# Later weight copies and squares, a reserve of channel matmuls, six raw buffers: a fused attention and mixer kernel on one Trainium2 core

## The chip, the core and the metric

The kernel runs on one core of a Trainium2 chip. A core has a matrix engine (TensorE, "PE" in the profile, with weight loads in a row of their own, "PEld"), a vector engine (VectorE, "DVE"), a scalar engine (ScalarE, "ACT"), GpSimd ("POOL") and SyncE ("SP"). Each works through its own list of instructions in order; between engines there are semaphores. PE reads SBUF and writes PSUM. PSUM is handed out in banks. Data comes from and goes to DRAM by DMA, which an engine issues and 16 DMA engines carry out.

The metric is the device time of one execution in microseconds (us). Lower is better.

## The reference

Eight batches, 12 heads, 448 tokens, head size 64. Attention without a softmax (squared ReLU of the scores) is followed by an MLP mixer: a token mix over the 448 tokens (hidden 256) and a channel mix over the 768 channels (hidden 1536).

```python
def _attn_ref(q, k, v):
    S = q.shape[2]
    scale = 1.0 / np.sqrt(q.shape[-1])
    scores = scale * np.matmul(q, k.transpose(0, 1, 3, 2))
    attn = np.maximum(scores, 0.0) ** 2 / S
    return np.matmul(attn, v)

def _moe_ref(x, w_tok1, w_tok2, w_ch1, w_ch2):
    xt = x.transpose(0, 2, 1)
    h = np.maximum(xt @ w_tok1, 0.0) @ w_tok2
    u = x + h.transpose(0, 2, 1)
    h2 = np.maximum(u @ w_ch1, 0.0) @ w_ch2
    return u + h2
```

All inputs and the output are float32 in DRAM; the kernel computes in bfloat16 with float32 sums, and the loads convert.

## The kernel before

**Pairs and iterations.** The unit of attention work is a pair of heads: six pairs a batch (`NP`), 48 pairs in all. The main loop (L399) runs over s = 0 to 51. In iteration s the work of several pairs is interleaved, so that each step's inputs were made some iterations earlier:

- scores of pair s: three blocks of 128 keys, each with both heads (`sc_ps`, L186), and the remaining 64 keys of both heads together (`sr_ps`, L200). For each block `relu2` (L172) puts a ReLU on ACT (`at`, L175) and a square on DVE (`sq`, L176);
- transposes of q and k of pair s+1 on PE (`qkT_ps`, L159) and the copy to `qkT` on DVE (L169), which the scores of iteration s+1 read;
- values of pair s-1 (`acc_ps`, L216 and L224) and the scaling into `xT` on DVE (L232);
- x_back of pair s-2: PE transposes `xT` (`x_ps`, L250), DVE copies it to `x_sb` (L258);
- for odd s token1, for even s token2, of two pairs at once (`PG` = 2): `t_ps` (L268) with a ReLU on ACT (L276), then `h_ps` (L286) and an add on DVE that makes `uT_sb` (L294).

**Order.** The order on each engine is the order in which the program emits instructions; nothing is rearranged (`manual_schedule`). An iteration emits: scores of blocks 0 and 1 with their ReLUs and squares; the loads of pair s+3; the weight loads due in this iteration; fill; x_back; token2; fill; scores of block 2; transposes; values; rest scores; fill; token1; fill.

**Channel work and fills.** When the last pair of a batch has had its token2 (s = 8, 14, 20, ... 50), `channel_work` puts the batch's channel matmuls into a list, as units: 12 units of channel1 (six matmuls L311 and a ReLU on ACT, L318) and six or eight units of channel2 (12 matmuls L329, three L339, an output copy on DVE, L347; six for an even batch, eight for an odd one). `fill(0.25)` is called four times an iteration. Each call adds 1186 ns to a credit (a quarter of the mean work of a batch over six iterations) and runs units while the credit is above zero, each at its assumed cost: 1134 ns for channel1, 2124 ns for channel2. With an empty list the credit is held at or below zero. After the loop the rest of the list is run.

**PSUM.** `ps_mm` has three banks, which `qkT_ps`, `x_ps`, `t_ps`, `h_ps` and the channel matmuls use in rotation; `ps_att` has two buffers of two banks for the scores, `ps_acc` one.

**Loads.** All loads stand in POOL's queue, in the order of emission. A pair's load is a q, a k and a v load (112, 96 and 96 KB in SBUF); the first pair of a batch adds four loads of the last 64 keys and values of all heads (`load_rest`, 48 KB each, into `kz` and `vz`). Pairs 0, 1 and 2 are loaded before the loop, pair s+3 in iteration s. The pool `raw` has four buffers of each kind, so the v load of pair n waits until the values matmuls of pair n-4 are done. The weights: wt1 at s=0 (seven loads), wt2 at s=1 (one load into `wt2_nat`, then two DVE copies, L125, that reorder it), wc1 in quarters at s=2 to 5, wc2 in quarters at s=6 to 9. The identity for the transposes is made by POOL, after the loads of pair 0 (L392). Outputs are stored from SP's queue.

Of the kernel before, what the change touches and what calls it, by code (L numbers as in the profile page):

```python
# [9 lines left out]
FP32 = mybir.dt.float32  # L10
BF16 = mybir.dt.bfloat16
AF = mybir.ActivationFunctionType
ALU = mybir.AluOpType
# [3 lines left out]
def kernel(  # L17
# [11 lines left out]
    nc = tc.nc  # L29
# [4 lines left out]
    DC = moe_w_ch1.shape[1]  # L34
# [15 lines left out]

    consts = ctx.enter_context(tc.tile_pool(name="consts", bufs=1))
    wpool = ctx.enter_context(tc.tile_pool(name="wpool", bufs=1))
    raw = ctx.enter_context(tc.tile_pool(name="raw", bufs=4))
    attn = ctx.enter_context(tc.tile_pool(name="attn", bufs=2))
    mix = ctx.enter_context(tc.tile_pool(name="mix", bufs=2))
    outp = ctx.enter_context(tc.tile_pool(name="outp", bufs=3))
# [2 lines left out]
    ps_mm = ctx.enter_context(tc.tile_pool(name="ps_mm", bufs=3, space=bass.MemoryType.PSUM))  # L59
# [3 lines left out]
    ident = consts.tile([128, 128], BF16, name="ident")  # L63
# [12 lines left out]
    def load_pair(s):  # L76
        b, p = divmod(s, NP)
        h0 = 2 * p
        q_raw = raw.tile([QP, 2, QC, D], BF16, name="q_raw")
        k_raw = raw.tile([128, 2, KB, D], BF16, name="k_raw")  # L80
        v_raw = raw.tile([128, 2, KB, D], BF16, name="v_raw")
        nc.gpsimd.dma_start(  # L82
            out=q_raw.rearrange("p h c d -> p h (c d)"),
            in_=q[b, h0 : h0 + 2].rearrange("h (p c) d -> p h (c d)", c=QC),
        )
        nc.gpsimd.dma_start(  # L86
            out=k_raw.rearrange("p h c d -> p h (c d)"),
            in_=k[b, h0 : h0 + 2, :KM].rearrange("h (p c) d -> p h (c d)", c=KB),
        )
        if p == 0:  # L90
            load_rest(b, kz[b % 2], k)
        nc.gpsimd.dma_start(  # L92
            out=v_raw.rearrange("p h c d -> p h (c d)"),
            in_=v[b, h0 : h0 + 2, :KM].rearrange("h (p c) d -> p h (c d)", c=KB),
        )
        if p == 0:
            load_rest(b, vz[b % 2], v)
        raws[s] = (q_raw, k_raw, v_raw)

    def load_rest(b, dst, src):  # L100
        for e in range(2):
            nc.gpsimd.dma_start(
                out=dst[64 * e : 64 * e + KR, :, D * e : D * (e + 1)],
                in_=src[b].rearrange("(p e) s d -> e s p d", e=2)[e, KM:],
            )

    def load_wt1():
        w = moe_w_tok1.rearrange("(p c) j -> c p j", c=QC)
        for c in range(QC):
            lo = c * QP  # L110
            while lo < (c + 1) * QP:
                hi = min((c + 1) * QP, (lo // 128 + 1) * 128)
                r = lo % 128
                nc.gpsimd.dma_start(
                    out=wt1[r : r + hi - lo, lo // 128, :],
                    in_=w[c, lo - c * QP : hi - c * QP, :],
                )
                lo = hi

    def load_wt2():  # L120
        nc.gpsimd.dma_start(
            out=wt2_nat, in_=moe_w_tok2.rearrange("(c j) s -> j c s", c=JC)
        )
        for j in range(JC):
            nc.vector.tensor_copy(  # L125
                wt2[:, j, :].rearrange("n (c p) -> n c p", c=QC),
                wt2_nat[:, j, :].rearrange("n (p c) -> n c p", c=QC),
            )

    def load_wc1(i):  # L130
        n = DC // 4
        nc.gpsimd.dma_start(
            out=wc1[:, :, i * n : (i + 1) * n],
            in_=moe_w_ch1.rearrange("(g p) n -> p g n", p=128)[:, :, i * n : (i + 1) * n],
        )

    def load_wc2(i):
        n = EC // 4
        nc.gpsimd.dma_start(
            out=wc2[:, i * n : (i + 1) * n, :],  # L140
            in_=moe_w_ch2.rearrange("(e p) n -> p e n", p=128)[:, i * n : (i + 1) * n, :],
        )


    qkT, at2, acc = {}, {}, {}
    KO = S

    def transposes(s):
# [23 lines left out]
    def relu2(s, key, ps, n):  # L172
        at = attn.tile([128, n, S], BF16, tag=f"at{n}", name="at", bufs=3)
        sq = attn.tile([128, n, S], BF16, tag=f"sq{n}", name="sq", bufs=3 * (3 if n == 2 else 1))
        nc.scalar.activation(at, ps[:, :, :S], AF.Relu)  # L175
        nc.vector.tensor_tensor(out=sq, in0=at, in1=at, op=ALU.mult)  # L176
        at2[s, key] = sq

    def scores(s, blocks):
        sb = qkT[s]  # L180
        made = []
        for c in blocks:
            ps = ps_att.tile([128, 2, 512], FP32, tag="att", name="sc_ps")
            for e in range(2):
                h = slice(64 * e, 64 * (e + 1))
                nc.tensor.matmul(  # L186
                    ps[:, e, :S],
                    lhsT=sb[h, KO + c * 128 : KO + (c + 1) * 128],
                    rhs=sb[h, :S],
                    start=True,  # L190
                    stop=True,
                )
            made.append((c, ps))
        for c, ps in made:
            relu2(s, c, ps, 2)

    def scores_rest(s):
        sb = qkT.pop(s)
        ps = ps_att.tile([128, 1, 512], FP32, tag="att", name="sr_ps")
        nc.tensor.matmul(  # L200
            ps[:, 0, :S],
            lhsT=sb[:, KO + KM : KO + KM + 128],
            rhs=sb[:, :S],
            start=True,
            stop=True,
        )
        relu2(s, KB, ps, 1)
# [36 lines left out]
    def x_back(s):  # L244
        b, p = divmod(s, NP)
        if p % PG == 0:
            x_tiles[s // PG] = mix.tile([128, 4, PG, 128], BF16, name="x_sb")
        ps = ps_mm.tile([128, 1024], BF16, tag="bank", name="x_ps")
        for c in range(4):
            nc.tensor.matmul(  # L250
                ps[:, c * 128 : (c + 1) * 128],
                lhsT=xT[b % 2][:, p, c * 128 : (c + 1) * 128],
                rhs=ident,
                is_transpose=True,
                start=(c == 0),
                stop=(c == 3),
            )
        nc.vector.tensor_copy(  # L258
            x_tiles[s // PG][:, :, p % PG, :],
            ps[:, :512].rearrange("n (c d) -> n c d", c=4),  # L260
        )
# [100 lines left out]
    queue = []  # L362

    def channel_work(b):
        for e in range(EC):
            queue.append((6 * 189, lambda e=e: channel1(b, e)))
        half = NT // 2
        for t in range(half) if b % 2 == 0 else range(half, NT):
            for i in range(2):
                queue.append((12 * 163 + 3 * 56, lambda t=t, i=i: channel2(b // 2, t, i)))  # L370

    NS = B * NP
    given = [0.0]
    credit = [0.0]
    per_batch = EC * 6 * 189 + NT * (12 * 163 + 3 * 56)

    def fill(share):
        credit[0] += share * per_batch / NP
        while queue and credit[0] > 0:
            cost, unit = queue.pop(0)  # L380
            credit[0] -= cost
            unit()
        if not queue:
            credit[0] = min(credit[0], 0.0)


    PRE = 3
    for i in range(2):
        nc.vector.memset(kz[i], 0.0)
        nc.vector.memset(vz[i], 0.0)  # L390
    load_pair(0)
    make_identity(nc, ident)  # L392
    for i in range(2):
        nc.vector.memset(xT[i][:, :, S:], 0.0)
    nc.vector.memset(wt1[:, 3, :], 0.0)
    load_pair(1)
    load_pair(2)
    transposes(0)
    for s in range(NS + 4):  # L399
        if s < NS:  # L400
            scores(s, (0, 1))
        if s + PRE < NS:
            load_pair(s + PRE)
        if s == 0:
            load_wt1()
        if s == 1:
            load_wt2()
        if 2 <= s < 6:
            load_wc1(s - 2)
        if 6 <= s < 10:  # L410
            load_wc2(s - 6)
        fill(0.25)
        if 0 <= s - 2 < NS:
            x_back(s - 2)
        if 0 <= s - 3 < NS and (s - 3) % PG == PG - 1:
            for i in range(PG):
                token2(s - 3 - (PG - 1) + i)
            if (s - 3) % NP == NP - 1:
                channel_work((s - 3) // NP)
        fill(0.25)  # L420
        if s < NS:
            scores(s, (2,))
        if s + 1 < NS:
            transposes(s + 1)
        if 0 <= s - 1 < NS:
            values(s - 1)
        if s < NS:
            scores_rest(s)
        fill(0.25)
        if 0 <= s - 2 < NS and (s - 2) % PG == PG - 1:  # L430
            token1((s - 2) // PG)
        fill(0.25)
# [32 lines left out]
```

## Time and profile before

| | before |
|---|---|
| median of 3 runs | 452.16 us (451.62 to 452.26) |
| profiled execution | 451.94 us |
| its span, first to last instruction | 450.2 us |
| PE busy | 408.8 us, 91% of the span |
| DVE busy | 231.0 us, 51% |
| ACT busy | 212.3 us, 47% |
| POOL busy | 132.6 us, 29% |
| loads, in POOL's queue | 21.70 MB as written to SBUF |
| stores, in SP's queue | 11.01 MB |

All times below come from the profiled execution, counted from its first instruction; 451.94 - 450.2 = 1.74 us lie outside the span. Matmuls overlap in the array, and the profile models their ends, so a run of matmuls is measured from start to start. Records on DVE overlap by some hundredths too. A timeline row reads: start, duration, engine, line, operation, tile written<-tiles read, sizes, count; in brackets, how long the engine stood idle before it and what ended the wait.

### The profile page before, as it was taken

How to read it: one execution, taken by the hardware profiler on the slowest of the kernel's cores; microseconds unless marked ns; L12 is line 12 of the kernel's file. 1: busy time of each engine (PE TensorE's matmuls, PEld its weight loads, DVE VectorE, ACT ScalarE, POOL GpSimd, SP SyncE). 2: the span in 40 equal slices, each digit the busy share in tenths (PEclk: the TensorE clock that was granted, in tenths of full speed). 3: DMA queues.
4: the chain of work that ended last, by engine and by line, in shares of the span. 5: the costliest groups of instructions: out<-in, count | busy, mean ns of one | idle time of the engine just before them, and what ended most of it. 6: DMA issues, size and time to landing. Idle time of an engine off the chain costs nothing.

```text
span 450.2 us, 8061 instructions
## 1 busy us (share of the span) xinstructions
PE 408.8 (91%) x3336; PEld 218.2 (48%) x3336; DVE 231.0 (51%) x449; ACT 212.3 (47%) x313; POOL 132.6 (29%) x198
## 2 busy tenths in 40 slices
PE   2467799998999989998999989999899989999995
PEld 1134344554455544554445545455445545455563
DVE  3278754565455655556446663555545565443011
ACT  3346756535653456534654337634564436630400
POOL 8837553312511333311431224113333110000000
PEclk9999999999999999999999999999999999999999
DMA  8939999543633635445455446336534532012013
GB/s 80 117 34 168 201 177 123 67 87 64 62 40 65 123 62 52 47 66 105 38 51 78 77 83 66 41 64 90 73 38 56 99 64 45 0 37 58 14 46 96
DMA packets 60517, 33.23 MB, mean 74 GB/s; under 512 B 40832, under 2 KB 56896, under 8 KB 60480
## 3 DMA queue, kind: packets, MB, share of 16 engines
q0 software_dynamic: 56000, 21.70, 43.2%
q1 hardware_dynamic: 4480, 11.01, 8.5%
q8 instruction: 26, 0.43, 0.4%
q14 instruction: 11, 0.09, 0.1%
HBM read 43.38 MB, written 11.01 MB: 121 GB/s over the span
## 4 chain that ended last, share of the span: by engine, by line
PE 77%; ACT 8%; issue 5%; DVE 4%; POOL 4%; DMA 1%; ACTq 0%; DVEq 0%; POOLq 0%
PE m_ps L311 23%; PE m_ps L329 22%; ACT at L175 7%; PE sc_ps L186 6%; PE acc_ps L216 6%; PE qkT_ps L159 5%; PE t_ps L268 4%; PE acc_ps L224 3%; PE m_ps L339 2%; PE h_ps L286 2%; PE sr_ps L200 2%; PE x_ps L250 1%; DVE sq L176 1%; DMA wt_nat<-in_moe_w_tok_dram 1%; DVE out_sb L347 1%
## 5 line engine op out<-in xcount | busy, mean ns | idle before, releaser
L176 DVE TENSOR_TENSOR sq<-at 128x896 bf16<-128x896 bf16 x192 | 108.4, 564 | 136.4 <-ACT at L175 136.4
L175 ACT ACTIVATE at<-sc_ps 128x896 bf16<-128x896 f32 x144 | 125.8, 917 | 84.1 <-PE sc_ps L186 84.1
L329 PE MATMUL m_ps<-wc,r_sb 128*128 128x384 bf16 x672 | 126.5, 326 | 4.6 <-DVE x_sb L258 4.6
L311 PE MATMUL m_ps<-uT_sb,wc 128*128 128x448 bf16 x576 | 120.6, 353 | 6.4 <-DVE x_sb L258 6.3
L92 POOL DMA_DIRECT2D v_raw<-in_v_dram x48 | 34.1, 711 | 233.8 <-PE acc_ps L224 215.3
L311 PEld LDWEIGHTS <-wc 128*128 128x128 bf16 x576 | 54.4, 98 | 61.8 <-issue 16.6
L318 ACT ACTIVATE r_sb<-m_ps 128x448 bf16<-128x448 f32 x96 | 52.5, 547 | 65.3 <-PE m_ps L311 65.3
L329 PEld LDWEIGHTS <-r_sb 128*128 128x128 bf16 x672 | 63.3, 98 | 39.0 <-issue 3.7
L347 DVE COPY out_sb<-m_ps 128x384 f32<-128x384 f32 x56 | 31.2, 556 | 64.5 <-PE m_ps L329 64.5
L186 PE MATMUL sc_ps<-qkT 64*128 64x448 bf16 x288 | 45.8, 369 | 13.0 <-DVE qkT L169 10.1
L175 ACT ACTIVATE at<-sr_ps 128x448 bf16<-128x448 f32 x48 | 26.1, 543 | 33.1 <-PE sr_ps L200 32.9
L216 PE MATMUL acc_ps<-sq,v_raw 128*64 128x448 bf16 x288 | 36.6, 362 | 0.0
L86 POOL DMA_DIRECT2D k_raw<-in_k_dram x48 | 34.9, 728 | 0.0
L169 DVE COPY qkT<-qkT_ps 128x960 bf16<-128x960 bf16 x48 | 31.3, 651 | 4.8 <-PE qkT_ps L159 4.8
L82 POOL DMA_DIRECT2D q_raw<-in_q_dram x48 | 32.7, 682 | 1.1 <-POOLq L449 0.8
L186 PEld LDWEIGHTS <-qkT 64*128 64x128 bf16 x288 | 11.1, 95 | 45.3 <-issue 28.8
L276 ACT ACTIVATE r_sb<-t_ps 128x512 bf16<-128x512 f32 x24 | 14.3, 597 | 33.6 <-PE t_ps L268 33.6
L232 DVE TENSOR_SCALAR xT<-acc_ps 128x448 bf16<-128x448 f32 x48 | 29.6, 616 | 0.7 <-PE acc_ps L224 0.7
L159 PE MATMUL qkT_ps<-ident,q_raw 112*64 112x112 bf16 x384 | 19.4, 225 | 9.3 <-POOL ident masks.py:199 6.8
L294 DVE TENSOR_TENSOR uT_sb<-h_ps,xT 128x448 bf16<-128x448 f32 x48 | 27.5, 615 | 0.0
L286 PE MATMUL h_ps<-wt,r_sb 128*128 128x448 bf16 x96 | 24.3, 352 | 3.3 <-ACT r_sb L318 2.5
L268 PE MATMUL t_ps<-x_sb,wt 128*128 128x256 bf16 x192 | 24.9, 273 | 0.0
(35 smaller groups left out, 265.7 us busy)
## 6 DMA issues: line engine op xcount, KB each, us to landing
q_raw<-in_q_dram POOLq DMA_DIRECT2D x48, 112.0 KB, 3.2
k_raw<-in_k_dram POOLq DMA_DIRECT2D x48, 96.0 KB, 3.3
v_raw<-in_v_dram POOLq DMA_DIRECT2D x48, 96.0 KB, 2.9
wc<-in_moe_w_ch_dram POOLq DMA_DIRECT2D x8, 576.0 KB, 7.2
out_dram<-out_sb SPq DMA_DIRECT2D x8, 336.0 KB, 2.8
out_dram<-out_sb SPq DMA_DIRECT2D x8, 288.0 KB, 2.9
out_dram<-out_sb SPq DMA_DIRECT2D x8, 240.0 KB, 2.8
out_dram<-out_sb SPq DMA_DIRECT2D x8, 192.0 KB, 2.9
```

What stands on the lines that cost most here:

```text
L86: nc.gpsimd.dma_start(out=k_raw.rearrange("p h c d -> p h (c d)"), in_=k[b, h0 : h0 + 2, :KM].rearrange("h (p c) d -> p h (c d)", c=KB),)
L92: nc.gpsimd.dma_start(out=v_raw.rearrange("p h c d -> p h (c d)"), in_=v[b, h0 : h0 + 2, :KM].rearrange("h (p c) d -> p h (c d)", c=KB),)
L159: nc.tensor.matmul(ps[64 * h : 64 * (h + 1), at : at + n], lhsT=src[:, h, :], rhs=ident[:n, :n], is_transpose=True, start=True, stop=True, ...
L175: nc.scalar.activation(at, ps[:, :, :S], AF.Relu)
L176: nc.vector.tensor_tensor(out=sq, in0=at, in1=at, op=ALU.mult)
L186: nc.tensor.matmul(ps[:, e, :S], lhsT=sb[h, KO + c * 128 : KO + (c + 1) * 128], rhs=sb[h, :S], start=True, stop=True,)
L216: nc.tensor.matmul(ps[64 * e : 64 * (e + 1), :S], lhsT=v_raw[:, e, c, :], rhs=sq[:, e, :], start=(c == 0), stop=False, skip_group_check=True,)
L268: nc.tensor.matmul(ps[:, j, :], lhsT=wt1[:, c, j * 128 : (j + 1) * 128], rhs=x_sb[:, c].rearrange("n g d -> n (g d)"), start=(c == 0), sto ...
L311: nc.tensor.matmul(ps[:, :S], lhsT=wc1[:, g, e * 128 : (e + 1) * 128], rhs=uT[:, g, off : off + S], start=(g == 0), stop=(g == CC - 1),)
L318: nc.scalar.activation(r2[:, e, off : off + S], ps[:, :S], AF.Relu)
L329: nc.tensor.matmul(ps[:, :HN], lhsT=r2[:, e, tok], rhs=wc2[:, e, cols], start=(e == 0), stop=(e == EC - 1), skip_group_check=True,)
L347: nc.vector.tensor_copy(o[:, cols], ps[:, :HN])
```

## The change

1. `raw` gets six buffers instead of four.
2. `make_identity` is called inside `load_pair(0)`, after the q and k loads of pair 0 and before the rest loads.
3. The reordering copies of wt2 leave `load_wt2` and become `order_wt2`, called at s=3. The load itself stays at s=1.
4. wc1 is loaded in two halves at s=3 and s=5; the quarters of wc2 go to s=7 to 10.
5. `relu2` no longer emits the square; it notes it, and `square()` emits those noted. It is called after x_back (squares of blocks 0 and 1) and after the rest scores (block 2 and the rest), so behind the qkT copy and the xT scaling.
6. The credit of `fill` starts at -2500 instead of 0, isn't changed while the list is empty, and is no longer held at zero.
7. Ahead of everything DVE clears a tile `warm`, and PE runs nine matmuls 128x512 on it, whose result isn't used.

```diff
-    raw = ctx.enter_context(tc.tile_pool(name="raw", bufs=4))
+    raw = ctx.enter_context(tc.tile_pool(name="raw", bufs=6))
...
+        if s == 0:
+            make_identity(nc, ident)
         if p == 0:
             load_rest(b, kz[b % 2], k)
...
+
+    def order_wt2():
         for j in range(JC):
             nc.vector.tensor_copy(
...
     def load_wc1(i):
-        n = DC // 4
+        n = DC // 2
...
         nc.scalar.activation(at, ps[:, :, :S], AF.Relu)
-        nc.vector.tensor_tensor(out=sq, in0=at, in1=at, op=ALU.mult)
+        squares.append((at, sq))
         at2[s, key] = sq
+
+    def square():
+        for at, sq in squares:
+            nc.vector.tensor_tensor(out=sq, in0=at, in1=at, op=ALU.mult)
+        squares.clear()
...
-    credit = [0.0]
+    RESERVE = 2500.0
+    credit = [-RESERVE]
...
     def fill(share):
+        if not queue:
+            return
         credit[0] += share * per_batch / NP
         while queue and credit[0] > 0:
             cost, unit = queue.pop(0)
             credit[0] -= cost
             unit()
-        if not queue:
-            credit[0] = min(credit[0], 0.0)
...
+    warm = consts.tile([128, 512], BF16, name="warm")
+    nc.vector.memset(warm, 0.0)
     for i in range(2):
         nc.vector.memset(kz[i], 0.0)
         nc.vector.memset(vz[i], 0.0)
+    warm_ps = ps_mm.tile([128, 512], FP32, tag="bank", name="warm_ps")
+    for i in range(9):
+        nc.tensor.matmul(warm_ps, lhsT=warm[:, :128], rhs=warm, start=True, stop=True)
     load_pair(0)
-    make_identity(nc, ident)
...
-        if 2 <= s < 6:
-            load_wc1(s - 2)
-        if 6 <= s < 10:
-            load_wc2(s - 6)
+        if s == 3:
+            order_wt2()
+        if s in (3, 5):
+            load_wc1((s - 3) // 2)
+        if 7 <= s < 11:
+            load_wc2(s - 7)
         fill(0.25)
         if 0 <= s - 2 < NS:
             x_back(s - 2)
+        square()
...
         if s < NS:
             scores_rest(s)
+        square()
         fill(0.25)
```

More of the change, by code (lines that the diff above doesn't have):

```diff
@@ L142, in load_wc2 @@
         )
-    qkT, at2, acc = {}, {}, {}
+    qkT, at2, squares = {}, {}, []
     KO = S
@@ L372 @@
     NS = B * NP
-    given = [0.0]
-    credit = [0.0]
+    RESERVE = 2500.0
+    credit = [-RESERVE]
     per_batch = EC * 6 * 189 + NT * (12 * 163 + 3 * 56)
     def fill(share):
+        if not queue:
+            return
         credit[0] += share * per_batch / NP
```

## The prediction

> **What bounds the kernel now.** I read the chain of work that ended last, then the waits, then the timeline of the places that the waits name.
>
> ```profile
> PE 77%; ACT 8%; issue 5%; DVE 4%; POOL 4%; DMA 1%; ACTq 0%; DVEq 0%; POOLq 0%
> ```
>
> TensorE (PE) holds 77% of the chain. So a gap of PE is worth its length, and work taken off another engine is worth only the PE gaps that it causes. The waits say which gaps there are:
>
> ```profile
> POOL v_raw L92 <- PE acc_ps L224: 215.3, 39, 8.9
> PE sc_ps L186 <- DVE qkT L169: 10.1, 5, 7.5
> DVE wt L125 <- DMA wt_nat<-in_moe_w_tok_dram: 7.7, 1, 7.7
> PE qkT_ps L159 <- POOL ident masks.py:199: 6.8, 1, 6.8
> PE m_ps L311 <- DVE x_sb L258: 6.3, 4, 1.7
> PE m_ps L329 <- DVE x_sb L258: 4.6, 3, 1.5
> ```
>
> Columns: total us, times, longest. PE waits once 7.5 us for a qkT copy, DVE once 7.7 us for a load, and PE seven times, 10.9 us in all, for VectorE's (DVE's) x_sb copy. The long POOL row is a queue held by four raw buffers; no PE wait for a q or k load stands among these, so by itself it costs nothing. First place, the timeline around 19 to 25 us (start, duration, engine, line):
>
> ```profile
> 8.55 0.93 PE L186 MATMUL sc_ps<-qkT 64*128 64x448 bf16 x4 [0.75 <-DVE qkT L169]
> ...
> 18.94 0.73 POOL L121 DMA_DIRECT2D wt_nat<-in_moe_w_tok_dram  x1
> 23.67 0.70 DVE L125 COPY wt<-wt_nat 128x448 bf16<-128x448 bf16 x2 [7.72 <-DMA wt_nat<-in_moe_w_tok_dram]
> 24.82 0.65 DVE L169 COPY qkT<-qkT_ps 128x960 bf16<-128x960 bf16 x1
> 25.53 0.93 PE L186 MATMUL sc_ps<-qkT 64*128 64x448 bf16 x4 [7.51 <-DVE qkT L169]
> 30.35 0.36 PE L186 MATMUL sc_ps<-qkT 64*128 64x448 bf16 x2
> ```
>
> In iteration s=1 the copies of wt2 stand in DVE's queue and wait for wt_nat; the qkT copy of s=2 is behind them, and PE waits for that. Second place, iteration s=6, before channel work exists:
>
> ```profile
> 34.77 0.55 PE L186 MATMUL sc_ps<-qkT 64*128 64x448 bf16 x4
> ...
> 44.48 0.55 PE L186 MATMUL sc_ps<-qkT 64*128 64x448 bf16 x4
> 46.69 0.62 DVE L176 TENSOR_TENSOR sq<-at 128x896 bf16<-128x896 bf16 x1 [0.18 <-ACT at L175]
> 47.23 0.42 DVE L258 COPY x_sb<-x_ps 128x512 bf16<-128x512 bf16 x1
> 47.57 1.15 DVE L294 TENSOR_TENSOR uT_sb<-h_ps,xT 128x448 bf16<-128x448 f32 x2
> 48.63 0.62 DVE L176 TENSOR_TENSOR sq<-at 128x896 bf16<-128x896 bf16 x1
> 49.16 0.65 DVE L169 COPY qkT<-qkT_ps 128x960 bf16<-128x960 bf16 x1
> 49.73 0.62 DVE L232 TENSOR_SCALAR xT<-acc_ps 128x448 bf16<-128x448 f32 x1
> 50.26 0.39 DVE L176 TENSOR_TENSOR sq<-at 128x448 bf16<-128x448 bf16 x1
> ```
>
> From scores to scores runs a DVE chain: two squares (the second at 46.69), x copy, two adds, third square, qkT copy. Third place, the start of a batch's channel work (s=14):
>
> ```profile
> 104.44 0.55 PE L186 MATMUL sc_ps<-qkT 64*128 64x448 bf16 x4
> 105.20 0.93 PE L286 MATMUL h_ps<-wt,r_sb 128*128 128x448 bf16 x4
> 106.79 0.62 DVE L176 TENSOR_TENSOR sq<-at 128x896 bf16<-128x896 bf16 x1 [0.18 <-ACT at L175]
> 107.33 0.41 DVE L258 COPY x_sb<-x_ps 128x512 bf16<-128x512 bf16 x1
> 107.80 1.41 PE L311 MATMUL m_ps<-uT_sb,wc 128*128 128x448 bf16 x6 [1.68 <-DVE x_sb L258]
> ```
>
> No unit was left for the first fill, so the token matmuls follow the scores at once; the x copy sits behind two squares, these behind ACT, and the next unit lacks its bank.
>
> **The change, part by part.** Sums are made on the profiled execution, 451.94 us with a span of 450.2; the median of the runs is 452.16.
>
> *Before s=3: nothing.* Identity goes up the POOL queue: transposes no longer wait 6.8 us for it, but the rest loads of k, v0 and the rest loads of v follow it, later by its two POOL instructions; the first transposes then end on the k rest instead. I take no gain. A loss is covered: after the change DVE needs wt_nat only at s=3, and POOL's order up to that load stays, so it lands at about 23.67 again. Even at the slow pace 25.53 to 30.35 (4.82 us an iteration) s=3 would start by 8.55 + 3 x 4.82 = 23.0. The warm-up memset and nine matmuls stand on engines that wait for the first loads. All this, and the removed wait for raw buffers, buys nothing up to here.
>
> *wt2 copies at s=3.* The wait is not removed, it is moved: DVE stops at s=3, and behind it stand the x copy, two squares and the qkT copy for s=4. From 23.67: copies 0.70, x copy 0.34, squares 2 x 0.54, qkT copy 0.65, 0.1 to PE gives 26.54 for the scores of s=4 (spacings of the rows of s=6). Before they were at 34.77: **-8.2**.
>
> *Squares later, s=4 to 7.* The third square (48.63 to 49.16: 0.53) leaves the chain to qkT, and the x copy (0.34) no longer follows the first two: 0.87 an iteration, 1.74 from 9.71 a pair (34.77 to 44.48), 7.97. DVE's own work in a pair is eight squares (six of 0.54, two of 0.39), two each of qkT (0.57), xT (0.53), x (0.34), adds of 1.06: 3.24 + 0.78 + 2.88 + 1.06 = 7.96, so the next bound is there at once; I take 8.1. Two pairs: 16.2; next are the rows of s=8:
>
> ```profile
> 54.15 0.55 PE L186 MATMUL sc_ps<-qkT 64*128 64x448 bf16 x4
> 57.38 2.55 PE L311 MATMUL m_ps<-uT_sb,wc 128*128 128x448 bf16 x12 [1.54 <-DVE x_sb L258]
> 61.65 2.43 PE L311 MATMUL m_ps<-uT_sb,wc 128*128 128x448 bf16 x12
> 64.02 0.55 PE L186 MATMUL sc_ps<-qkT 64*128 64x448 bf16 x4
> ```
>
> Before, 34.77 to 54.15 is 19.4: **-3.2**. S=8 starts at 42.7. If DVE's queue has a wait that I miss, half of this goes.
>
> *Reserve at s=8.* The credit starts at -2500 and a fill grants 1186, so of s=8's fills only the fourth (the third that grants work after the batch is queued) runs a unit. Before, s=8 took 9.87 with four units of 2.37/2 = 1.19. After: second square ends 2.8 after the scores (46.69 + 0.54 - 44.48), adds end 3.9, one unit 1.2: 5.1. The three units left are done later, 3.6. 5.1 + 3.6 - 9.87 = **-1.2**.
>
> *Loads that run ahead.* POOL now passes pairs 5 and 6 early, and wc1 goes out in two halves.
>
> ```profile
> 40.00:50.00 10.00, 7.54 (x82) 3.95 (x83) 8.42 (x18) 6.92 (x10) 6.82 (x10) 1.00 1.30 183
> 60.00:70.00 10.00, 10.00 (x90) 4.96 (x89) 5.02 (x10) 6.89 (x11) 5.33 (x8) 1.00 1.19 160
> wc<-in_moe_w_ch_dram POOLq DMA_DIRECT2D x8, 576.0 KB, 7.2
> ```
>
> The queue is worked off in order. Behind wt_nat (23.67), up to k of pair 9, by the shapes: five pairs' worth of q, k, v less one v (1.46 MB), four rest loads (0.20) and all of wc1 (2.36): 4.0 MB. At 183 GB/s (last column, weight loads in flight) that is 22 us: 45.6; at 160 it is 48.7. The transposes for s=9 stand in front of values, rest scores and the first unit (1.75 us of PE) and would want pair 9 by 42.7 + 3.9 - 1.75 = 44.9. I take **+0.7**; the ends are 0 and +3.8. The Trainium skill, "DMA: Bandwidth & Descriptors", section "Anatomy of one DMA", gives 2.0 us plus bytes over 436 GB/s, which would land 576 KB in 3.4 us; the row has 7.2, and by that figure of the Trainium skill pair 9 would be early and the sum 432.0.
>
> *Batch boundaries.* Seven waits for x_sb make 10.9; less the 1.54 of s=8, 9.4 in six, 1.56 each. From s=20 on the first fill has a channel2 unit in hand: credit stands at about -1563 when a batch has been worked off, and the 24 fills of a batch end in the boundary's first fill with one more unit to run. That gives ACT and DVE its 2.1 us (12 x 163 + 3 x 56 ns, the source's own cost), and the x copy is no longer behind squares. Next late is the second token matmul, whose bank is that unit's, freed by its out copy:
>
> ```profile
> 91.48 1.20 PE L286 MATMUL h_ps<-wt,r_sb 128*128 128x448 bf16 x4
> ```
>
> 1.20 against the 0.93 at 105.20: 0.27. So 5 x (1.56 - 0.27) = **-6.5**. At s=14 there is no reserve: batch 0 has 6 + 12 units, 26352 ns of work against 28476 - 2500 granted, so its last unit runs one fill early and the queue is empty. There PE passes on to the third scores, transposes and values (some 1.8 us) and then waits for the adds; half of the wait stays: **-0.8**.
>
> *Elsewhere*, the squares now wait behind the x copy, which waits for PE's fill; behind them stand the adds that free two of three banks. One unit of fill (1.19) and the third scores stand before the bank is wanted, two squares take 1.08: I take nothing. The wait for credit itself costs nothing, since PE has no gaps in the tail after s=50 and the reserved units only move there.
>
> Sum: -8.2 - 3.2 - 1.2 + 0.7 - 6.5 - 0.8 = -19.2; 451.94 - 19.2 = **432.7**.
>
> **The rivals.**
> *Cold array.* Scores at 25.53 take 0.93, at 34.77 0.55, though the granted clock is full:
>
> ```profile
> PEclk9999999999999999999999999999999999999999
> ```
>
> Token1 at the full pace is this row:
>
> ```profile
> 53.05 1.03 PE L268 MATMUL t_ps<-x_sb,wt 128*128 128x256 bf16 x8
> ```
>
> So PE runs at about half pace up to 30.35, some 4.8 us after it starts to be busy. If it is still so in s=3, PE ends s=3 at 23.0 + 4.8 = 27.8, token1 at twice 1.03 ends at 29.9, and s=4 starts 3.3 later: 436.0. For it: between the nine matmuls and the scores at 8.55 PE has only transposes. Against: PE is busier from 8.55 to 23 than before. The Trainium skill, "TensorE: Matmul & The Clock Gate", Part 1, says that full rate comes after about 3.4 us of sustained work and is lost after an idle window as long; by that rule the nine matmuls could be undone before the scores begin, which is this rival; the trace agrees with the length of the run-up (4.8 us at 25.53) and with the loss after 7.51 us of waiting, and shows nothing in between.
>
> *Late loads.* At 160 GB/s pair 9 comes at 48.7: +3.1, 435.8.
>
> *Boundaries stay.* If the stall comes back behind another bank holder, the 7.3 are lost: 440.0. For it: only three banks, and ACT's order is unchanged. Against: the reserve puts a whole unit in between.
>
> *Slower.* In each of 20 even iterations from s=10 on the adds are two squares (1.08) later; were all of that a PE gap, 21.6 us would go, 454.3. It decides from 0.96 us an iteration. Against it is the cover named above.
>
> *Not what it says.* The reserve is absent at the first boundary, worked out above; if it is absent at all, 439.2.
>
> **How the numbers follow.** Forecast 0.55 (428 to 435); cold array or late loads 0.2 (436); boundaries stay, in whole or part, 0.18 (437 to 440); slower 0.03; better than 428, 0.04. A run can tell 0.2% (0.9 us) from no change. Faster 0.95, same 0.02, slower 0.03. Range: below, no cost of loads and all boundaries without wait (0.7 + 1.4 + 0.8) and as much again in small waits, 427; above, boundaries stay with half the late loads, 442.
>
> **What would show it.** DVE's wt2 copies start at about 23.7 with a wait of some 2 to 3 us, scores of s=4 at 26.5, of s=8 at 42.7; no PE wait for x_sb over 1 us after s=14; a POOL row of waits for acc_ps that has another place. A long PE wait for q_raw or k_raw at 36 to 48 means late loads; scores of 0.93 after 24 us a cold array; new PE waits for uT_sb in even iterations would make the prediction wrong.

## The result and the profile after

The changed kernel takes 428.64 us (median of four runs, 427.96 to 429.84) against 451.89 us before (median of four, 451.58 to 452.26): a ratio of 0.9488, 95% interval 0.9462 to 0.9514. That is 23.3 us less; 19.2 were forecast, to 432.7. The profiled execution took 429.84 us with a span of 428.0, 22.1 us less than the span before. Line numbers have moved: scores L195, transposes L163 and their copy L173, squares L185, x_back L259 and L267, token1 L277, token2 L295 and L303, channel1 L320, channel2 L338.

The page of the changed kernel, the granted clock by fortieths of the span, then the shares of the chain:

```profile
PEclk8699899999999999999999999999999999999999
...
PE 85%; ACT 4%; POOL 4%; DVE 3%; issue 2%; DMA 1%; ACTq 0%; DVEq 0%; POOLq 0%
```

And its waits, the rows that answer to those of before (total us, times, longest):

```profile
POOL v_raw L94 <- PE acc_ps L233: 177.5, 31, 8.5
...
PE sc_ps L195 <- DVE qkT L173: 3.9, 6, 1.1
...
DVE wt L129 <- DMA wt_nat<-in_moe_w_tok_dram: 1.9, 1, 1.9
```

The clock row dips in the first two slices (up to 21 us) and in the fifth (43 to 54 us); it was full throughout before. PE's share of the chain went from 77% to 85%. The waits of channel matmuls for x_sb (10.9 us in seven) are gone altogether. The wait for the qkT copy fell from 10.1 to 3.9 us, DVE's wait for wt_nat from 7.7 to 1.9. POOL still waits 177.5 us for values: two more buffers moved that wait, and behind the start no PE wait for a load goes with it in either profile.

Where the 22.1 us came from is seen by setting the starts of the same scores side by side. These are the timeline's rows for s=4, 8 and 9 of the changed kernel, and DVE's copies of wt2:

```profile
24.35 0.70 DVE L129 COPY wt<-wt_nat 128x448 bf16<-128x448 bf16 x2 [1.89 <-DMA wt_nat<-in_moe_w_tok_dram]
...
27.07 0.55 PE L195 MATMUL sc_ps<-qkT 64*128 64x448 bf16 x4 [0.60 <-DVE qkT L173]
...
46.11 0.55 PE L195 MATMUL sc_ps<-qkT 64*128 64x448 bf16 x4
...
50.90 0.55 PE L195 MATMUL sc_ps<-qkT 64*128 64x448 bf16 x4
```

| stretch | before, us | after, us | difference | forecast |
|---|---|---|---|---|
| up to the scores of s=4 | 34.77 | 27.07 | -7.7 | -8.2 |
| s=4 to s=8 | 19.38 | 19.04 | -0.3 | -3.2 |
| s=8, with its three units fewer (3.56) added | 9.87 | 8.35 | -1.5 | -1.2 |
| late loads | | | 0 | +0.7 |
| s=9 to the end, the three units taken off | 386.15 | 373.58 | -12.6 | -7.3 |
| sum | | | -22.1 | -19.2 |

Two terms are off: s=4 to 8 brought almost nothing in this execution, and the long part behind it brought five more than forecast. The experiments take the change apart with both in mind.

### The profile page after: what moved, and what is told of

Same layout as the page of the kernel before. It is cut to its first block, busy times and chain, and to the rows that moved or that the text cites. A ratio compares the mean times of both kernels' runs of the same rounds, so it can differ in the third digit from the quotient of the medians.

```text
span 428.0 us, 8076 instructions
## 1 busy us (share of the span) xinstructions
PE 410.1 (96%) x3345; PEld 218.7 (51%) x3345; DVE 230.0 (54%) x450; ACT 212.7 (50%) x313; POOL 130.8 (31%) x196
## 4 chain that ended last, share of the span: by engine, by line
PE 85%; ACT 4%; POOL 4%; DVE 3%; issue 2%; DMA 1%; ACTq 0%; DVEq 0%; POOLq 0%
PE m_ps L338 26%; PE m_ps L320 24%; PE sc_ps L195 7%; PE acc_ps L225 6%; PE qkT_ps L163 5%; PE t_ps L277 5%; ACT at L179 3%; PE h_ps L295 3%; PE acc_ps L233 3%; PE m_ps L348 2%; PE sr_ps L209 2%; PE x_ps L259 2%; DMA wt_nat<-in_moe_w_tok_dram 1%; DVE out_sb L356 1%; POOL wt L116 1%
## 5 line engine op out<-in xcount | busy, mean ns | idle before, releaser
L338 PE MATMUL m_ps<-wc,r_sb 128*128 128x384 bf16 x672 | 126.2, 326 | 0.0
L320 PE MATMUL m_ps<-uT_sb,wc 128*128 128x448 bf16 x576 | 120.4, 353 | 0.0
L185 DVE TENSOR_TENSOR sq<-at 128x896 bf16<-128x896 bf16 x192 | 100.6, 560 | 4.7 <-ACT at L179 4.6
L94 POOL DMA_DIRECT2D v_raw<-in_v_dram x48 | 34.5, 719 | 189.6 <-PE acc_ps L233 177.5
L338 PEld LDWEIGHTS <-r_sb 128*128 128x128 bf16 x672 | 63.4, 98 | 39.4 <-issue 4.1
L320 PEld LDWEIGHTS <-wc 128*128 128x128 bf16 x576 | 54.1, 98 | 53.8 <-issue 8.2
L267 DVE COPY x_sb<-x_ps 128x512 bf16<-128x512 bf16 x48 | 20.2, 422 | 66.6 <-PE x_ps L259 66.6
L195 PE MATMUL sc_ps<-qkT 64*128 64x448 bf16 x288 | 45.4, 364 | 6.7 <-DVE qkT L173 3.9
L173 DVE COPY qkT<-qkT_ps 128x960 bf16<-128x960 bf16 x48 | 31.4, 654 | 21.8 <-PE qkT_ps L163 21.7
L195 PEld LDWEIGHTS <-qkT 64*128 64x128 bf16 x288 | 10.8, 94 | 38.6 <-issue 27.7
L303 DVE TENSOR_TENSOR uT_sb<-h_ps,xT 128x448 bf16<-128x448 f32 x48 | 27.6, 616 | 0.0
L295 PE MATMUL h_ps<-wt,r_sb 128*128 128x448 bf16 x96 | 24.3, 352 | 2.8 <-ACT r_sb L327 2.5
L277 PE MATMUL t_ps<-x_sb,wt 128*128 128x256 bf16 x192 | 25.7, 278 | 0.9 <-DVE x_sb L267 0.9
```

What stands on the lines that cost most here:

```text
L94: nc.gpsimd.dma_start(out=v_raw.rearrange("p h c d -> p h (c d)"), in_=v[b, h0 : h0 + 2, :KM].rearrange("h (p c) d -> p h (c d)", c=KB),)
L195: nc.tensor.matmul(ps[:, e, :S], lhsT=sb[h, KO + c * 128 : KO + (c + 1) * 128], rhs=sb[h, :S], start=True, stop=True,)
L277: nc.tensor.matmul(ps[:, j, :], lhsT=wt1[:, c, j * 128 : (j + 1) * 128], rhs=x_sb[:, c].rearrange("n g d -> n (g d)"), start=(c == 0), sto ...
L295: nc.tensor.matmul(ps[:, :S], lhsT=r1[:, j, (p % PG) * 128 : (p % PG + 1) * 128], rhs=wt2[:, j, :], start=(j == 0), stop=(j == JC - 1),)
L320: nc.tensor.matmul(ps[:, :S], lhsT=wc1[:, g, e * 128 : (e + 1) * 128], rhs=uT[:, g, off : off + S], start=(g == 0), stop=(g == CC - 1),)
L338: nc.tensor.matmul(ps[:, :HN], lhsT=r2[:, e, tok], rhs=wc2[:, e, cols], start=(e == 0), stop=(e == EC - 1), skip_group_check=True,)
```

## Experiments

All are variants of the changed kernel but one, which is the kernel before with a single part. Each was timed beside the kernel before on the same chip (medians of before 451.4 to 451.8 us).

### The reserve undone

```diff
-    credit = [-RESERVE]
+    credit = [0.0]
...
-        if not queue:
-            return
...
+        if not queue:
+            credit[0] = min(credit[0], 0.0)
```

> The changed kernel with the old credit rule (start at 0, held at or below zero while the list is empty). Theory: the batch starts lost their PE waits to two things, the unit in reserve and the x copy that no longer stands behind squares. Without the reserve the second fill of a boundary runs a unit at once. At s=20, 32, 44 that is a channel2 unit of the old batch, which only wants a bank, and the early x copy frees one: no wait. At s=8, 14, 26, 38 it is a channel1 unit, which wants the last adds: a PE wait for uT_sb of some 1.3 us each. Time 428.6 + 4 to 5 = 433. Rival 1, the reserve alone did it: waits of 1.5 us at all seven, 438 to 440. Rival 2, the squares alone did it: 429, no PE wait over 0.5 us.

Measured: 435.79 us (433.92 to 436.09), ratio 0.9641 (0.9619 to 0.9663). The PE waits of this kernel, and its timeline at s=26, where channel1 is next, and at s=20, where a channel2 unit is:

```profile
PE m_ps L320 <- DVE uT_sb L303: 4.9, 8, 1.1
```

```profile
196.91 0.92 PE L295 MATMUL h_ps<-wt,r_sb 128*128 128x448 bf16 x4
197.66 0.92 PE L320 MATMUL m_ps<-uT_sb,wc 128*128 128x448 bf16 x4
199.56 0.35 PE L320 MATMUL m_ps<-uT_sb,wc 128*128 128x448 bf16 x1 [0.98 <-DVE uT_sb L303]
```

```profile
146.62 0.92 PE L295 MATMUL h_ps<-wt,r_sb 128*128 128x448 bf16 x4
147.38 0.33 PE L338 MATMUL m_ps<-wc,r_sb 128*128 128x384 bf16 x1
```

The picture is the one that the theory drew. With a bank freed early the unit starts at once in both; the channel1 unit runs four matmuls and stops for the last two adds, the channel2 unit doesn't stop. The waits stand in pairs at s=8, 14, 26 and 38 and nowhere else. The median is 2.8 us above the forecast, the profiled execution (433.92) 0.9. Each place costs 1.1 to 1.3 and then 0.34 us of PE starts, 6.2 in four places, not 1.3 each. That is also how far its span, 432.1, lies above that of the kernel without warm-up matmuls below (425.9), whose s=7 kept its pace like this one's. The other three runs are some 2 us longer; no profile of one was kept.

### The squares put back

```diff
-        squares.append((at, sq))
+        nc.vector.tensor_tensor(out=sq, in0=at, in1=at, op=ALU.mult)
```

> The changed kernel with every square emitted right behind its ReLU again. Theory: s=4 to 7 go back to a chain with the third square and the x copy in it, +3.2 us (0.87 an iteration); the unit in reserve still covers the boundaries from s=20, s=14 gets back some 1 us, and the small waits for x_sb (0.18 at seven places) come back, 1.3: 434, between 432 and 436. Rival 1, the order of squares carries the boundaries too: 440 to 443. Rival 2, late loads of pair 9 and the cold array set s=8 anyway: 430.

Measured: 442.10 us (441.98 to 442.22), ratio 0.9789 (0.9775 to 0.9804): rival 1, and 8 us off the theory. PE's waits for x_sb, and the place where the channel matmuls have theirs, s=18 (PE's rows, then DVE's):

```profile
PE m_ps L338 <- DVE x_sb L267: 7.7, 5, 1.5
PE qkT_ps L163 <- DVE x_sb L267: 5.0, 4, 1.3
```

```profile
129.45 0.55 PE L195 MATMUL sc_ps<-qkT 64*128 64x448 bf16 x4
...
130.17 0.92 PE L295 MATMUL h_ps<-wt,r_sb 128*128 128x448 bf16 x4
132.63 0.32 PE L338 MATMUL m_ps<-wc,r_sb 128*128 128x384 bf16 x1 [1.54 <-DVE x_sb L267]
```

```profile
130.80 0.63 DVE L180 TENSOR_TENSOR sq<-at 128x896 bf16<-128x896 bf16 x1 [0.69 <-ACT at L179]
131.61 0.62 DVE L180 TENSOR_TENSOR sq<-at 128x896 bf16<-128x896 bf16 x1 [0.18 <-ACT at L179]
132.16 0.42 DVE L267 COPY x_sb<-x_ps 128x512 bf16<-128x512 bf16 x1
```

The reserve does put a unit into the boundary's first fill. But a channel2 unit costs 2124 and a fill grants 1186, so some first fill goes empty, and with the reserve that is the one of s=18, 24, 30, 36 and 42. The wait comes back there with the same 1.54 us. The same iteration in the changed kernel, PE and then DVE:

```profile
126.93 0.55 PE L195 MATMUL sc_ps<-qkT 64*128 64x448 bf16 x4
...
127.64 0.92 PE L295 MATMUL h_ps<-wt,r_sb 128*128 128x448 bf16 x4
128.40 0.33 PE L338 MATMUL m_ps<-wc,r_sb 128*128 128x384 bf16 x1
```

```profile
127.85 0.43 DVE L267 COPY x_sb<-x_ps 128x512 bf16<-128x512 bf16 x1 [0.25 <-PE x_ps L259]
128.28 0.63 DVE L185 TENSOR_TENSOR sq<-at 128x896 bf16<-128x896 bf16 x1
```

No unit in the first fill here either, and no wait: the x copy comes first and frees the bank. So the order of squares removes the wait for the bank, wherever the empty fill falls; the reserve removes the other wait, for uT_sb, by not running a unit right behind token2. Each alone leaves the other: undone, they cost 7.2 and 13.5 us, together more than the 12.6 that s=9 to the end gained: neither cure is whole without the other, and the squares also carry some 2.9 us of the start in that profile (s=9 began at 51.69 there, at 48.78 in the kernel without warm-up matmuls; neither has the half pace told of below). From s=9 to the end the kernel before took 386.15 us, this one with the reserve alone 385.0 (its three later units taken off), the one above with the order of squares alone 378.4, and both together 373.58: the reserve alone won 1.1 us there, the order alone 7.8.

### The copies of wt2, from both sides

Undone in the changed kernel:

```diff
-        if s == 3:
+        if s == 1:
             order_wt2()
```

> The changed kernel with the two copies of wt2 on DVE at s=1 again. Theory: DVE stops at s=1 until the load lands at about 24 us, scores of s=2 start at about 25.5 and s=4 some 6 to 7 us later than the 27.07 of the changed kernel: 428.6 + 6 = 434.5 (433 to 436). Rival, the loads of pairs 7 and 9 or the rate of the array set s=8 in both: +1 to +3, 430 to 432.

Measured: 436.69 us (436.42 to 438.06), ratio 0.9677 (0.9657 to 0.9698), 8 us above the changed kernel; its profiled span is 6.9 us longer, and that difference stands from s=5 to the end unchanged. The median is 0.7 above the range that was expected. One row of its timeline, the scores of s=2:

```profile
25.13 0.93 PE L195 MATMUL sc_ps<-qkT 64*128 64x448 bf16 x4 [8.08 <-DVE qkT L173]
```

Alone, in the kernel before:

```diff
+        if s == 3:
+            order_wt2()
```

> The kernel before with one part alone: the two copies of wt2 on DVE at s=3 instead of s=1. Theory: the 7.5 us of PE wait become about 2, s=4 starts at 27 to 28 instead of 34.77, the rest of the start keeps its pace of 4.85 an iteration, v loads hold POOL as before: 452 - 7 = 445 (443.5 to 446.5). Rival: the four buffers and the third square take half of it back, 448.

Measured: 444.72 us (444.62 to 444.75), ratio 0.9841 (0.9829 to 0.9854), 7.0 less, as the theory had it. Its scores of s=4 and its PE waits, with those for x_sb as in the kernel before:

```profile
27.59 0.55 PE L188 MATMUL sc_ps<-qkT 64*128 64x448 bf16 x4
```

```profile
PE m_ps L313 <- DVE x_sb L260: 6.3, 4, 1.7
PE m_ps L331 <- DVE x_sb L260: 4.6, 3, 1.5
```

The start and the boundaries are two separate matters, and this part is worth 7 to 8 us in either surrounding.

### The warm-up matmuls left out

```diff
-    warm = consts.tile([128, 512], BF16, name="warm")
-    nc.vector.memset(warm, 0.0)
...
-    warm_ps = ps_mm.tile([128, 512], FP32, tag="bank", name="warm_ps")
-    for i in range(9):
-        nc.tensor.matmul(warm_ps, lhsT=warm[:, :128], rhs=warm, start=True, stop=True)
```

> The changed kernel without the tile warm and the nine matmuls on it. Theory: they buy nothing, since the iterations before s=3 are covered by the wait for wt_nat, and the array is at half pace again at 9.2 us with them: 428.6 within 0.7, scores of s=4 at about 27. Rival, they save the start 1 us or more of half pace that reaches the end: 429.6 to 432, scores of s=3 later than 23.

Measured: 428.06 us (427.69 to 429.24), ratio 0.9483 (0.9467 to 0.9499). They buy nothing. But its profile is of use: its span is 425.9 us, 2.12 less than that of the changed kernel. Of these, 0.49 us stand at the scores of s=4 already (26.58 against 27.07); the other 1.63 are made in s=7. First the changed kernel's s=7 up to token1 (the scores of s=8 follow at 46.11), then this one's scores of s=4 and its s=7 up to the scores of s=8:

```profile
40.34 0.55 PE L195 MATMUL sc_ps<-qkT 64*128 64x448 bf16 x4 [1.08 <-DVE qkT L173]
...
42.46 1.21 PE L225 MATMUL acc_ps<-sq,v_raw 128*64 128x448 bf16 x6
...
43.94 0.58 PE L209 MATMUL sr_ps<-qkT 128*128 128x448 bf16 x1
44.32 1.86 PE L277 MATMUL t_ps<-x_sb,wt 128*128 128x256 bf16 x8
```

```profile
26.58 0.55 PE L195 MATMUL sc_ps<-qkT 64*128 64x448 bf16 x4 [0.59 <-DVE qkT L173]
...
39.85 0.55 PE L195 MATMUL sc_ps<-qkT 64*128 64x448 bf16 x4 [1.08 <-DVE qkT L173]
...
41.97 0.73 PE L225 MATMUL acc_ps<-sq,v_raw 128*64 128x448 bf16 x6
...
42.83 0.35 PE L209 MATMUL sr_ps<-qkT 128*128 128x448 bf16 x1
43.02 1.04 PE L277 MATMUL t_ps<-x_sb,wt 128*128 128x256 bf16 x8
43.99 0.55 PE L195 MATMUL sc_ps<-qkT 64*128 64x448 bf16 x4
```

In the changed kernel's profile the array fell back to half pace in s=7: the rest scores and token1 start 0.38 us apart there, 0.19 here. That was the cold array of the prediction's rival, four iterations later than it was looked for.

### PE kept busy in the start

```diff
+        for i in range(7 if s in (4, 6) else 1):
+            nc.tensor.matmul(
+                ps[:, 0, :S],
...
+            if s in (5, 7) and c == 1:
+                for e in (0, 1, 0, 1):
```

> The changed kernel with matmuls repeated where PE waits before channel work exists: the rest scores of s=4 and s=6 seven times instead of once, the second score block of s=5 and s=7 three times. They write the same values. Theory: the half pace at 42 to 45 us in the profile of the changed kernel (s=7) comes of PE being too little busy before, and is 2.1 us of its time in those runs that have it; kept busy, token1 of s=7 takes 0.9 instead of 1.7 in every run and the runs agree at about 426.3 + 1.7 = 428.0 or, with the added matmuls partly in the way, 428.5, with no run over 429. Rival: the half pace does not depend on that; runs spread from 428 to 430.5 as before.

Measured: 428.64 us (428.25 to 429.04), ratio 0.9494 (0.9478 to 0.9510). Token1 of s=7 took 1.04 in its profile and scores of s=8 began at 44.93, 0.9 later than without the repeats. The four runs lie within 0.8 us where the changed kernel's lay within 1.9, which agrees with the theory, though one run lies just above the 429 that it allowed; four runs don't settle it, and the repeats cost what they save.

### Loads: four buffers, and wt2 ahead

```diff
-    raw = ctx.enter_context(tc.tile_pool(name="raw", bufs=6))
+    raw = ctx.enter_context(tc.tile_pool(name="raw", bufs=4))
```

> The changed kernel with four raw buffers. Theory: POOL is held again by the v loads, pair 9 comes 1 to 2 us later and the transposes of s=8 wait for it; after that nothing: 428.6 + 1 (0 to 2.5). Rival 1: buffers gave nothing, 428.6 within 0.4. Rival 2: run-ahead is what the early start lives on, 433 or more.

Measured: 428.68 us (427.59 to 430.22), ratio 0.9498 (0.9471 to 0.9524): no difference from six buffers that can be told. The transposes of s=6 and s=8 do wait for loads in its profile, 1.5 us the longest; its s=7 ran at full pace, which gave that back. Beside a profile of the changed kernel that kept its pace as well (the one told of at "A version with a shorter start", span 426.1) its span, 428.4, is 2.4 us longer. The medians don't show that, so what the two buffers are worth stays open.

```diff
         if s == 0:
+            load_wt2()
             load_wt1()
-        if s == 1:
-            load_wt2()
```

> The changed kernel with the load of wt2 moved from s=1 to s=0, ahead of the loads of wt1, so that DVE finds it at s=3. Theory: the 1.9 us that DVE waits at s=3 go, scores of s=4 start at about 25 instead of 27, but pairs 7 and 9 land when they landed (k at 37.0 and 46.9) and stop the transposes of s=6 and s=8: PE waits for q_raw or k_raw of 1 to 3 us in all, and the time stays within 0.7 of 428.6. Rival: nothing else is near, 426.7.

Measured: 429.47 us (428.63 to 430.86), ratio 0.9516 (0.9491 to 0.9540): nothing won; the median is 0.9 us above 428.6, where the theory had 0.7 at most. The scores of s=4 began at 24.78, 2.3 us earlier, and then the timeline has these transposes for pairs 7 and 9:

```profile
38.17 0.39 PE L163 MATMUL qkT_ps<-ident,q_raw 112*64 112x112 bf16 x8 [0.98 <-DMA q_raw<-in_q_dram]
...
47.09 0.39 PE L163 MATMUL qkT_ps<-ident,q_raw 112*64 112x112 bf16 x8 [0.70 <-DMA q_raw<-in_q_dram]
```

So the late loads of the prediction are real and lie at or just behind the path that the changed kernel takes. (Its profile has the half pace too, at s=5, as told at the end.)

As wt2_early, with the halves of wc1 behind pairs 7 and 9:

```diff
-        if s in (3, 5):
+        if s in (4, 6):
```

> As wt2_early, and the halves of wc1 at s=4 and s=6 instead of 3 and 5, behind the loads of pairs 7 and 9. Theory: with the pairs ahead of the weights in POOL's queue the 1.9 us are kept: 426.5, no PE wait for q_raw or k_raw after 20 us. Rival: DVE's own work bounds s=3 to 8 anyway, 428 to 429.

Measured: 428.87 us (427.45 to 429.96), ratio 0.9502 (0.9470 to 0.9534). Its profiled span is 426.4, 1.7 less than the changed kernel's, but the runs don't show a gain, and the 426.5 of the theory was missed; pair 8, now behind the first half, stopped the transposes of s=7 (0.67 us for q_raw).

### A version with a shorter start

The changed kernel again, on the same chip as the next two:

> The changed kernel as it is, for the same chip as the next three. 428.6, runs between 427.9 and 430, in two groups some 2 us apart if the half pace at 42 us comes and goes.

427.92 us (427.84 to 429.64), ratio 0.9479 (0.9463 to 0.9495). Its profile (427.85 us, span 426.1) has no half pace in s=7. So s=8 comes earlier, and there the transposes for pair 9 do wait for their load:

```profile
43.53 0.55 PE L195 MATMUL sc_ps<-qkT 64*128 64x448 bf16 x4
...
45.86 0.39 PE L163 MATMUL qkT_ps<-ident,q_raw 112*64 112x112 bf16 x8 [0.35 <-DMA q_raw<-in_q_dram]
...
48.93 0.55 PE L195 MATMUL sc_ps<-qkT 64*128 64x448 bf16 x4
```

From s=8 to s=9 it takes 5.40 us where the first profile, without that wait, took 4.79.

Then wt2 ahead of wt1 and the halves of wc1 behind pairs 8 and 9:

```diff
-        if s in (3, 5):
-            load_wc1((s - 3) // 2)
+        if s in (5, 6):
+            load_wc1(s - 5)
```

> The changed kernel with wt2's load at s=0 ahead of wt1 and the halves of wc1 at s=5 and s=6, behind pairs 8 and 9. Theory: with each pair ahead of the weights that stood before it, no transposes wait over 0.5 us for q or k after 20 us; s=8 starts at 42.5 to 43 where the array keeps its pace (43.99 without the half pace in the changed kernel's kind), so 426.7 in such runs and 428.7 in the others. Rival: the pairs still come late because the loads as a whole are at their limit up to s=8, 428 to 429.5.

Measured: 426.39 us, ratio 0.9464 (0.9431 to 0.9496); four of the six runs lie between 426.10 and 426.48, as the theory had it (426.7), two at 430.1 and 430.5, 4 us above where 2 were expected. No profile of such a run was kept. The last one adds some repeats:

```diff
+        for i in range(4 if s in (4, 6) else 1):
...
+            if s in (5, 7) and c == 1:
+                for e in (0, 1):
```

> As start_a, with the rest scores of s=4 and 6 four times instead of once and the second score block of s=5 and 7 twice, the same values each time, to keep PE busy. Theory: the half pace at s=7 stays away in all runs, 426.5 to 427.3, and the runs agree within 1 us. Rival: the half pace moves to another iteration or the repeats cost what they save, 428 or more.

Measured: 426.41 us (425.70 to 427.71 in five runs), ratio 0.9446 (0.9429 to 0.9464). It is the best of all in its ratio, 1.5 us below the changed kernel on that chip, with intervals that just touch. Its runs spread over 2.0 us where the theory had 1, so that the repeats hold the pace in every run is not shown. The scores of s=8 in its profile:

```profile
42.49 0.55 PE L195 MATMUL sc_ps<-qkT 64*128 64x448 bf16 x4
```

That is 3.6 us earlier than in the changed kernel's first profile, and the span, 424.4, is 3.6 shorter: an earlier s=8 is kept to the end. Of these, 1.6 are the half pace of that profile. Beside the second one it is 1.0 us earlier at s=8 and 1.6 shorter at the end; the 0.6 between is the wait for pair 9.

## Why the prediction was right, and where not

**wt2 copies at s=3: right.** The wait moved as described, to 24.35 from 23.67 (the load itself landed 0.7 later), and s=4 came at 27.07 instead of 26.54. Undone it costs 8.0 us, alone it brings 7.0.

**Before s=3: right.** Leaving out the nine matmuls changes nothing. The placing of the identity and the earlier clearing weren't tried alone.

**Squares, s=4 to 7: the mechanism right, the next bound wrong.** The prediction took DVE's own work, 8.1 us a pair. Without the half pace (the kernel without warm-up matmuls) s=4 to s=8 took 43.99 - 26.58 = 17.4, so 2.0 of the 3.2 came. The rest is in the odd iterations. Of DVE's 7.96 us a pair, 4.51 belong to an even iteration, with the adds, and 3.45 to an odd one. The even ones took about that, 4.48 (s=4) and 4.66 (s=6); the odd one of s=5 took 4.13:

```profile
32.92 0.37 PE L195 MATMUL sc_ps<-qkT 64*128 64x448 bf16 x2 [0.44 <-ACT at L179]
...
34.25 0.65 DVE L173 COPY qkT<-qkT_ps 128x960 bf16<-128x960 bf16 x1
...
34.71 1.04 PE L277 MATMUL t_ps<-x_sb,wt 128*128 128x256 bf16 x8
...
35.68 0.55 PE L195 MATMUL sc_ps<-qkT 64*128 64x448 bf16 x4
```

The qkT copy was done at 34.90; the scores of s=6 came 0.8 later, behind PE's own list: third scores behind ACT's first ReLU, transposes, values, rest scores, token1. "What is late next" was PE itself, and the prediction had looked at DVE alone: the scores of s=6 came at 35.68, where the chain over DVE would have been done at 35.0.

**Cold array: a rival in the prediction at the wrong place.** It asked whether s=3 would run at half pace; behind its first scores s=3 didn't (its token1 took 1.04 us). But s=7 did in this execution, 1.6 us. The windows of the changed kernel (PE busy first, granted clock third from the end):

```profile
35.00:40.00 5.00, 4.26 (x45) 1.96 (x43) 4.28 (x9) 4.03 (x6) 2.87 (x5) 1.00 1.42 197
40.00:45.00 5.00, 4.21 (x38) 2.05 (x39) 4.51 (x10) 2.97 (x4) 2.03 (x3) 0.76 1.20 206
...
42.60:45.90 3.30, 3.30 (x18) 1.52 (x12) 2.56 (x5) 1.23 (x2) 0.00 (x0) 0.50 1.33 195
```

The Trainium skill, "TensorE: Matmul & The Clock Gate", Part 1, has the full rate lost after an idle window of about 3.4 us. PE had no idle time over 1.1 us here in the 10 us before, so this trace doesn't agree with it as a rule on gaps. The same page of the Trainium skill, Part 4, says that transposes don't count as PE work in the same way. Leaving them out, PE still had no empty stretch over 1.1 us in these 10 us. And the second profile of the changed kernel has the same waits ahead of its s=7 (1.09 and 0.45 us) and kept its pace. So what set off the fall in the first profile stays open.

**Reserve at s=8: right** in size, -1.5 for -1.2. **Late loads: right as a mechanism, at the edge of costing.** Pair 9 was due to stop s=8 by 0.7 us. In the first profile s=8 itself came late, by the half pace, so nothing waited; in the second, with s=8 at 43.53, the wait cost 0.6; in the kernel without warm-up matmuls, with s=8 at 43.99, nothing waited. With a faster start (wt2_early) pair 9 stopped PE at s=8, and pair 7 at s=6 as well.

**Batch boundaries: the largest error, in size and in part in cause.** Forecast -7.3, measured -12.6. Three things make it up. The wait was priced by idle time behind modelled ends (1.56); from start to start of matmuls it is 1.7, and the new wait of 0.27 that was taken off took the place of an equal one at s=18. At s=14 the whole wait of 1.8 went, not half. Its timeline in the changed kernel, DVE's two adds, the rest scores and the first channel matmuls:

```profile
97.18 1.15 DVE L303 TENSOR_TENSOR uT_sb<-h_ps,xT 128x448 bf16<-128x448 f32 x2
...
97.65 0.35 PE L209 MATMUL sr_ps<-qkT 128*128 128x448 bf16 x1
97.84 2.43 PE L320 MATMUL m_ps<-uT_sb,wc 128*128 128x448 bf16 x12
```

A channel1 unit reads the pairs one by one, so it could start before the second add was done at 98.3; the prediction had it wait for both. And the small waits in ordinary even iterations, 0.18 at seven places, which the prediction left unpriced, went too. Together that is 5 x 1.70 + 1.84 + 7 x 0.18 = 11.6 of the 12.6. As to the cause, the prediction named both the reserve's unit in the first fill and the earlier x copy, and let its sum rest on the unit; with the squares put back that unit was there and the wait had moved to s=18. It is the order of squares that removes it.

**Slower, and adds that come later: excluded.** No PE wait for uT_sb over 0.2 us stands in the changed kernel's even iterations.

**The total: in part luck.** It came within 4 us because two errors have opposite signs: the boundaries brought 5.3 us more than forecast, s=4 to 8 brought 2.9 less, of which 1.6 are the half pace. The profiled execution without the half pace took 427.85 us, just below the 428 to 435 that had the largest chance.

## What to carry to other kernels

In a queue that is worked in order, look at what stands behind an instruction that waits: a copy that frees a bank belongs ahead of work that waits for another engine, and a copy that waits for a load belongs where its result is needed. If a remedy only fills the place of the stall (a unit in reserve), ask where the next empty place is; here it won little without the reordering. After taking one chain out, walk through every engine's list for the next bound, the busiest engine's first.

## What the runs showed of the hardware

The array can fall back to half pace in the middle of a kernel, with PE idle for no more than 1.1 us at a time: matmuls of token1 took 1.86 us in place of 1.04, for 1.6 us in all, in one of two profiles of the changed kernel and in neither's later iterations. With the wt2 copies back at s=1 it came at s=7 too, with the load of wt2 ahead at s=5 instead:

```profile
51.47 1.62 PE L277 MATMUL t_ps<-x_sb,wt 128*128 128x256 bf16 x8
```

```profile
33.65 1.63 PE L277 MATMUL t_ps<-x_sb,wt 128*128 128x256 bf16 x8
```

The granted clock doesn't always tell of it: it read 1.00 through the kernel before, whose matmuls took 0.93 for 0.55 up to 30 us; at s=7 of the changed kernel it does tell, with 0.50 from 42.6 to 45.9 us.
